# Copies, a gelu's scaling and row sums moved from VectorE to ScalarE in a one-core decode kernel

## The chip, the core and the metric

The kernel runs on one core of a Trainium2 chip. The metric is device microseconds of one execution, as the median of a few runs. All arithmetic is float32.

## What is computed

One decode step of a transformer block for 4 batch rows of one token each, width 512. The reference, cut to its core:

```python
mod = (silu(c) @ w_mod).reshape(4, 6, 1, 512)          # sa, ca, ga, sb, cb, gb
h = layernorm(x) * (1 + ca) + sa
q = (h @ wq) -> (4, 32 heads, 1, 128)
scores = q . k_cache * 128**-0.5                        # 8 kv heads, each for 4 q heads, 4096 keys
p = softmax(scores)
o = p . v_cache
x = x + ga * (o @ wo)                                   # wo: 4096 x 512
h = layernorm(x) * (1 + cb) + sb
z = layernorm(h)                                        # over the 512 columns
u = gelu(z[b, d] * w1[f] + b1[f])                       # f: 1792 hidden values per (b, d)
y = u . w2 + b2
out = x + gb * y
```

The key and value caches are 4 x 8 pairs of 2 MB + 2 MB, 134 MB together; with `w_mod`, `wq` and `wo` the kernel reads 157 MB.

## The kernel before

**Rows.** The work is cut into 32 rows `i`, one for each batch row `b = i // 8` and kv head `h = i % 8`. For row `i` the steps are small functions, each with a letter in the plan below:

- `scores` (line 226, PE): eight 512-wide matmuls into a PSUM tile `s` of 128 x 1024. The pool `ps_s` has two such buffers; the one of row `i` is free for row `i + 2` once the exponential of `i` has read it.
- the maximum: `row_max` on VectorE (line 236), `turn_max` (a transposition by PE into `pm`, line 240), `col_max` on VectorE (line 245), `spread_max` (PE into `pb`, line 251), and `copy_max` (line 256), which copies the 128 x 1 result from PSUM to the tile `nm`.
- `expo` (line 261, ScalarE): exponential with `nm` as bias, and with the sum of each partition accumulated; `turn` (VectorE, 32 x 32 block transpositions, whole at line 267 or in halves at line 271); `sums` (PE, `pl`, line 275) and `scale` (VectorE, reciprocal, line 280).
- `values` (PE, `pv`, line 291; the last rows use the narrow form at line 303), then `copy_v` (line 314), which copies the 128 x 512 result from PSUM to `po`; `pick` (PE, `pt`, line 328) and `copy_o` (VectorE, `oT`, line 335).
- `project` (PE with `wo`, `pa`, line 343) and `add_up` (line 359 copies the first projection of a batch row into `acc`, line 361 adds the others).

`pm`, `pb`, `pl`, `pt`, `pa` and the statistics `pst` share two PSUM buffers of the pool `ps_m`, in the order in which the program names them: each new one waits until the one two before has been read.

**Loads.** Keys and values come through a ring of three slots of 4 MB (`ring`), in pairs of keys `i + 2` and values `i`, all issued on SP's queue; a slot is loaded again once PE has consumed its values.

**The mixer.** The second half of the block for batch row `b` (class `Mixer`) runs beside the attention rows of `b + 1`. `expand` (VectorE, line 442) writes `hb * wr[:, j] + b1[:, j]` for two of 14 column groups `j` into a tile `u` of 128 x 1024, `gelu` (ScalarE, line 506) is applied to it, `consume` contracts it on PE (line 453). In the loop `both` does `expand` and `gelu`: in the rows with `i % 8` of 3 to 5 once between the two halves of `values` and in those of 2 to 5 once behind them. Mixers 0 and 1 run in the loop over rows 0 to 23. Mixer 2 runs in the plan below and mixer 3 in the closing sequence (`finish`); these use `expand` and `gelu` as separate steps.

**Gating of the last row.** The last batch row's residual is accumulated by PE itself: the `wo` columns of kv heads 6 and 7 are multiplied in place by the gate `ga` (`fold_gate`, line 592, letter `f`, eight products of 128 x 512), and the sum of each product goes into a column of `rowsum`, from which the mean for the layer norm is made.

**Order.** The order of the instructions on each engine is the order in which the program calls these functions (a manual schedule); each engine takes its list in order. Rows 0 to 23 come from the loop at line 618. From row 24 on the order is written out by hand in `PLAN` (line 667): for example `b31` is `spread_max(31)`, `B31` `copy_max(31)`, `e31` `expo(31)`, `t` a half of `turn`, `v` a quarter or half of `values`, `x` expand, `g` gelu, `c` consume, `f` one step of `fold_gate`, `L` followed by letters loads.

Of the kernel before, what the change touches and what calls it, by code (L numbers as in the profile page):

```python
# [8 lines left out]
F32 = mybir.dt.float32  # L9
AF = mybir.ActivationFunctionType  # L10
OP = mybir.AluOpType
# [3 lines left out]
B, D, HQ, HKV, SK, DH, F = 4, 512, 32, 8, 4096, 128, 1792  # L15
REP = HQ // HKV
NF = F // 128
EPS = 1e-5
P = 128
NS = B * HKV  # L20
# [8 lines left out]
def adaln_decode(ctx: ExitStack, tc: tile.TileContext, small, x, wmod, wq, kk, kv, vv, wo, out):  # L29
    nc = tc.nc  # L30
# [5 lines left out]
    up = ctx.enter_context(tc.tile_pool(name="up", bufs=3))  # L36
# [6 lines left out]
    dv = nc.vector  # L43
# [13 lines left out]
    w1, b1, w2 = sm[:, 0:NF], sm[:, NF:2 * NF], sm[:, 2 * NF:3 * NF]  # L57
# [34 lines left out]
    wo_t = [wo_p[h // 2][:, h % 2] for h in range(HKV)]  # L92
# [34 lines left out]
    for k in range(4):  # L127
        n = slice(k * P, (k + 1) * P)
# [95 lines left out]
    S, M, PL, RL = {}, {}, {}, {}  # L224
# [28 lines left out]

    def copy_max(i):
        nm = wk.tile([P, 1], F32, name="nm")
        dv.tensor_copy(nm, M[i])  # L256
        M[i] = nm

    def expo(i):
# [23 lines left out]
    PV, PA = {}, {}  # L283
# [27 lines left out]
    def copy_v(i):  # L311
        pv = PV[i]
        PV[i] = wk.tile(list(pv.shape), F32, name="po")
        dv.tensor_copy(PV[i], pv)  # L314

    ACC, OT = {}, {}

# [37 lines left out]
    def add_up(i):  # L355
        b, pa = i // HKV, PA.pop(i)
        if i % HKV == 0:
            ACC[b] = wk.tile([P, D], F32, name="acc", tag="acc", bufs=1)
            dv.tensor_copy(ACC[b], pa)
        else:  # L360
            dv.tensor_add(ACC[b], ACC[b], pa)  # L361

# [93 lines left out]
    class Mixer:  # L456
# [49 lines left out]
            nc.scalar.activation(u, u, AF.Gelu_apprx_tanh)  # L506
            self.done.append((u, js))

        def both(self, u=None):
            self.expand(u)  # L510
            self.gelu()

        def consume(self, most=9):
            if self.py is None:
# [65 lines left out]
    def spread_gate():  # L580
        pgb = ps_m.tile([P, 4, P], F32, name="pgb", tag="m")
        for c in range(4):
            e = 32 * c + 8 * (B - 1)
            mm(pgb[:, c, :], ident[:, e:e + 1].to_broadcast([P, P]), prep[:, 1], start=True, stop=True)
        gate = wk.tile([P, D], F32, name="gate", tag="yw", bufs=1)
        nc.scalar.activation(gate, pgb.rearrange("p c n -> p (c n)"), AF.Copy)
        return gate

    def fold_gate(gate, es):
        for e in es:  # L590
            w = wo_t[HKV - 2 + e // REP][:, e % REP]
            dv.tensor_tensor_reduce(w, w, gate, 1.0, 0.0, OP.mult, OP.add, rowsum[:, e:e + 1])

    rowsum = cst.tile([P, 2 * REP], F32, name="rowsum")
    tally = cst.tile([P, 2], F32, name="tally")
    both = cst.tile([P, 2 * REP], F32, name="both")
    mu = cst.tile([P, 1], F32, name="mu")

    def tally_up():
        junk = cst.tile([P, 2 * REP], F32, name="junk")  # L600
        dv.tensor_tensor_reduce(junk, both, rowsum, 1.0, tally[:, 0:1], OP.mult, OP.add, tally[:, 1:2])
# [10 lines left out]
    for i in range(2):  # L612
        for step in (scores, row_max, turn_max, col_max, spread_max, copy_max, expo):
            step(i)
# [3 lines left out]
    for i in range(NS - HKV):  # L618
# [13 lines left out]
        if i:  # L632
            project(i - 1)
            add_up(i - 1)
        turn_max(i + 2)
        col_max(i + 2)
        values(i, range(4))
        spread_max(i + 2)
        copy_max(i + 2)
        expo(i + 2)  # L640
        if i and i % HKV == 0:
            mix = Mixer(i // HKV - 1)
        if mix:
            mix.inner(i % HKV)
        values(i, range(4, 8))
        copy_v(i)
        if mix:
            mix.outer(i % HKV)
# [8 lines left out]
        if i == NS - HKV - 2:  # L657
            gate = spread_gate()
# [16 lines left out]
    g T2 zs za zx zq c c zm zb0 T3 zv zb1 zw0 zn zc  # L675
    """
    TABLE = {"s": scores, "S": row_max, "m": turn_max, "X": col_max, "b": spread_max, "B": copy_max, "e": expo,
             "l": sums, "L": scale, "V": copy_v, "a": pick, "A": copy_o, "P": add_up,
             "LP": load_pair}
    MIX = {"F": mix.fold, "R": mix.residual, "G": mix.gather, "M": mix.modulate, "H": mix.gather, "Q": mix.spread,  # L680
# [3 lines left out]
    for step in PLAN.split():  # L684
        op, k = step.rstrip("0123456789."), step.lstrip("abcdefghijklmnopqrstuvwxyzABCDEFGHIJKLMNOPQRSTUVWXYZ")
        i, q = (int(n) for n in (k + ".0").split(".")[:2]) if k else (0, 0)
# [25 lines left out]
        elif op == "x":  # L712
            mix.expand(spare if mix.n == 6 else None)
        elif op == "f":
            fold_gate(gate, gates[:1])
            del gates[:1]
        elif step == "T":
# [71 lines left out]
```

## Time and profile before

| | us |
|---|---|
| median of 3 runs | 386.43 |
| lowest and highest of them | 386.31, 390.96 |
| span of the profiled execution, first to last instruction | 384.7 |

| engine | busy us | share of the span |
|---|---|---|
| PE matmuls | 298.7 | 78% |
| PE weight loads | 117.2 | 30% |
| VectorE (DVE) | 198.2 | 52% |
| ScalarE (ACT) | 112.2 | 29% |
| GpSimd (POOL) | 7.7 | 2% |

The three runs and the profiled execution are separate executions; the span leaves out what lies around the first and the last instruction. In the page, PEld is PE's weight loading, which overlaps its matmuls, and "idle before" gives the time that an engine stood before an instruction and what released it. In the order of time a row reads: start, duration, engine, line, operation, output<-input, sizes, count, and in brackets the idle time with its releaser. In a stretch the columns are the busy time and count of PE, PEld, DVE, ACT, POOL, then the granted clock of PE, the DMA engines' mean busy share and their GB/s.

### The profile page before, as it was taken

Reading aid. Unit: us, or ns where it says so; the run is one execution under the profiler, and the core shown is the slowest. Engines: PE = TensorE matmul, PEld = TensorE weight load, DVE = VectorE, ACT = ScalarE, POOL = GpSimd, SP = SyncE. Lnnn points to the kernel's source line nnn. Section 1 sums busy time; section 2 is a strip of 40 time slices with the busy share of each in tenths; the row PEclk is TensorE's granted clock in tenths of the full one; section 3 lists DMA queues with packets and bytes.
Section 4 is the critical chain, followed back from the end, with each engine's and each line's share of the span. In section 5 each row is a group of like instructions: output and inputs, shape, how many; then the busy total and the mean of one; then the engine's idle time right before and its main releaser. Section 6 shows DMA issues by size and latency. Waiting matters only on the chain.

```text
span 384.7 us, 5604 instructions
## 1 busy us (share of the span) xinstructions
PE 298.7 (78%) x2380; PEld 117.2 (30%) x2380; DVE 198.2 (52%) x407; ACT 112.2 (29%) x144; POOL 7.7 (2%) x33
## 2 busy tenths in 40 slices
PE   0856777866966949979877878788888887999984
PEld 0112122311323313334322222342222343333653
DVE  1130251620451424664866545557665567778757
ACT  1001111121110110212567311124575105657276
POOL 1100000000000000000000000000000000000000
PEclk9989555985695685998999998999999999999999
DMA  8999999999999999999999999999999999999930
GB/s 331 433 433 436 411 453 433 409 432 436 423 441 433 434 436 436 434 436 431 429 425 433 428 433 434 429 433 431 429 434 436 434 436 432 424 417 423 418 122 3
DMA packets 7409, 157.69 MB, mean 410 GB/s; under 512 B 964, under 2 KB 1236, under 8 KB 1496
## 3 DMA queue, kind: packets, MB, share of 16 engines
q1 hardware_dynamic: 7376, 157.33, 95.4%
q8 instruction: 18, 0.29, 0.3%
q14 instruction: 7, 0.06, 0.0%
q10 hardware_dynamic: 8, 0.00, 0.0%
HBM read 157.32 MB, written 0.01 MB: 409 GB/s over the span
## 4 chain that ended last, share of the span: by engine, by line
DMA 60%; PE 29%; DVE 7%; ACT 2%; issue 1%; POOL 0%; SPq 0%; POOLq 0%; DVEq 0%
DMA kv<-in_kv 58%; PE s L231 8%; PE pv L291 7%; PE s L122 2%; PE qs L138 2%; DVE m L236 2%; DVE p L267 2%; DMA sm<-in_small 2%; PE pa L343 2%; PE pt L328 2%; ACT uu L562 1%; PE pb L251 1%; PE pve L303 1%; PE pm L240 1%; PE pgx L348 1%
## 5 line engine op out<-in xcount | busy, mean ns | idle before, releaser
L231 PE MATMUL s<-kv,QT 128*32 128x512 f32 x512 | 75.2, 714 | 38.9 <-DMA kv<-in_kv 37.0
L236 DVE TENSOR_REDUCE m<-s 128x1 f32<-128x1024 f32 x32 | 39.2, 1224 | 96.0 <-PE s L231 95.9
L261 ACT ACTIVATE p<-s,nm 128x1024 f32<-128x1024 f32 x32 | 35.7, 1115 | 180.6 <-DVE nm L256 180.5
L291 PE MATMUL pv<-kv,p 128*32 128x512 f32 x464 | 69.8, 670 | 0.7 <-DMA kv<-in_kv 0.7
L231 PEld LDWEIGHTS s<-kv,QT 128*32 128x32 f32 x512 | 15.8, 123 | 84.0 <-DMA kv<-in_kv 52.5
L328 PEld LDWEIGHTS pt<-g,po 128*128 128x128 f32 x236 | 31.1, 205 | 27.2 <-issue 19.9
L343 PE MATMUL pa<-wo,oT 128*32 128x512 f32 x240 | 34.6, 648 | 4.6 <-DVE oT L335 4.4
L328 PE MATMUL pt<-g,po 128*128 128x4 f32 (+2 forms) x236 | 33.9, 267 | 1.5 <-DVE po L314 1.0
L267 DVE STREAM_TRANSPOSE p<-p 128x1024 f32<-128x1024 f32 x25 | 30.9, 1234 | 0.0
L314 DVE COPY po<-pv 128x512 f32<-128x512 f32 x29 | 20.0, 688 | 16.8 <-PE pv L291 16.7
L245 DVE TENSOR_REDUCE mx<-pm 1x128 f32<-1x512 f32 x32 | 21.3, 669 | 1.1 <-PE pm L240 1.1
L442 DVE TENSOR_SCALAR u<-hb,wr,sm 128x512 f32<-128x512 f32 x40 | 19.9, 541 | 1.9 <-POOL wr L437 1.0
L506 ACT ACTIVATE u<-u 128x1024 f32<-128x1024 f32 x20 | 20.4, 1051 | 1.5 <-DVE u L442 1.4
L361 DVE TENSOR_TENSOR acc<-acc,pa 128x512 f32<-128x512 f32 x26 | 17.8, 686 | 4.3 <-PE pa L343 4.2
L261 ACT ACT_TABLE_LOAD x11 | 14.1, 1283 | 20.3 <-DVE nm L256 20.2
L251 PEld LDWEIGHTS pb<-neg,mx 1*128 1x128 f32 x64 | 10.4, 202 | 28.2 <-DVE mx L245 26.5
L122 PE MATMUL s<-wm,sT 128*4 128x512 f32 x16 | 9.1, 732 | 10.6 <-DVE sT L108 10.6
L506 ACT ACT_TABLE_LOAD x13 | 16.7, 1283 | 0.2
L291 PEld LDWEIGHTS pv<-kv,p 128*32 128x32 f32 x464 | 13.4, 146 | 7.2 <-issue 3.1
L240 PE MATMUL pm<-ident,m 128*1 128x128 f32 x32 | 9.3, 289 | 7.4 <-DVE m L236 3.5
L251 PE MATMUL pb<-neg,mx 1*128 1x1 f32 x64 | 13.1, 271 | 2.1 <-DVE mx L245 2.1
L453 PE MATMUL py<-u,sm 128*32 128x512 f32 x80 | 14.4, 616 | 0.0
(158 smaller groups left out, 214.7 us busy)
## 6 DMA issues: line engine op xcount, KB each, us to landing
kv<-in_kv SPq DMA_DIRECT2D x28, 4096.0 KB, 21.9
wq<-in_wq SPq DMA_DIRECT2D x2, 4096.0 KB, 16.3
wo<-in_wo SPq DMA_DIRECT2D x4, 2048.0 KB
kv<-in_kv SPq DMA_DIRECT2D x4, 2048.0 KB, 20.3
wm<-in_wmod SPq DMA_DIRECT2D x2, 2048.0 KB, 14.8
kv<-in_kk SPq DMA_DIRECT2D x1, 4096.0 KB
kv<-in_vv SPq DMA_DIRECT2D x3, 1024.0 KB
wm<-in_wmod SPq DMA_DIRECT2D x1, 1024.0 KB
```

The costliest lines, as they stand in the source:

```text
L231: mm(s[32 * c:32 * c + 32, n * 512:(n + 1) * 512], QT[:, b, h, :], KT[i][:, (n * 4 + c) * 512:(n * 4 + c + 1) * 512], start=True, stop=True)
L236: dv.tensor_reduce(M[i], S[i], axis=AX.X, op=OP.max)
L245: dv.tensor_reduce(mx, M[i].rearrange("o (c r) -> o r c", c=4).unsqueeze(1).to_broadcast([1, 4, 32, 4]), axis=AX.X, op=OP.max)
L251: mm(pb, M[i].rearrange("o c r -> o (c r)"), neg1, start=True, stop=True)
L261: nc.scalar.activation(p, S[i], AF.Exp, bias=M.pop(i), accum_out=l)
L267: dv.transpose(PL[i][0], PL[i][0])
L291: mm(PV[i][32 * q:32 * q + 32, :], pT[:, 128 * k:128 * k + 128:4], VT[i][:, 4 * k:4 * k + 4, :].rearrange("p j d -> p (j d)"), start=(k < ...
L314: dv.tensor_copy(PV[i], pv)
L328: mm(pt, po[:, c * DH:(c + 1) * DH], sel.unsqueeze(1).to_broadcast([P, m, REP]), start=(c == 0), stop=(c == n - 1))
L343: mm(pa[32 * g:32 * g + 32, :], oT[:, g:g + 1].to_broadcast([P, 32]), wo_t[h][:, g, :], start=True, stop=True)
L442: dv.tensor_scalar(u[:, e, :], hb, wr[:, j:j + 1], b1[:, j:j + 1], op0=OP.mult, op1=OP.add)
L506: nc.scalar.activation(u, u, AF.Gelu_apprx_tanh)
```

## The change

- `copy_max` (all 32 rows) runs on ScalarE.
- `copy_v` runs on ScalarE in rows 0 to 23; rows 24 to 31 stay on VectorE.
- The copy of the first projection of a batch row in `add_up` runs on ScalarE.
- `both` (mixers 0 and 1) no longer expands on VectorE: ScalarE applies gelu straight to `hb`, two instructions of 128 x 512 with `wr[:, j]` as scale and `b1[:, j]` as bias.
- `fold_gate`: in the first four of the eight steps VectorE multiplies two column groups (128 x 1024) by the gate, and in every step ScalarE copies one group of 128 x 512 in place and accumulates its sum. Before, each step was one product with sum on VectorE.

```diff
     def copy_max(i):
         nm = wk.tile([P, 1], F32, name="nm")
-        dv.tensor_copy(nm, M[i])
+        nc.scalar.activation(nm, M[i], AF.Copy)
         M[i] = nm
...
         PV[i] = wk.tile(list(pv.shape), F32, name="po")
-        dv.tensor_copy(PV[i], pv)
+        if i < NS - HKV:
+            nc.scalar.activation(PV[i], pv, AF.Copy)
+        else:
+            dv.tensor_copy(PV[i], pv)
...
         if i % HKV == 0:
             ACC[b] = wk.tile([P, D], F32, name="acc", tag="acc", bufs=1)
-            dv.tensor_copy(ACC[b], pa)
+            nc.scalar.activation(ACC[b], pa, AF.Copy)
...
-        def both(self, u=None):
-            self.expand(u)
-            self.gelu()
+        def both(self):
+            u = up.tile([P, 2, D], F32, name="u")
+            js = (2 * self.n, 2 * self.n + 1)
+            for e, j in enumerate(js):
+                nc.scalar.activation(u[:, e], self.hb, AF.Gelu_apprx_tanh, bias=b1[:, j:j + 1],
+                                     scale=self.wr[:, j:j + 1])
+            self.done.append((u, js))
+            self.n += 1
...
     def fold_gate(gate, es):
-        for e in es:
-            w = wo_t[HKV - 2 + e // REP][:, e % REP]
-            dv.tensor_tensor_reduce(w, w, gate, 1.0, 0.0, OP.mult, OP.add, rowsum[:, e:e + 1])
+        for n in es:
+            if n < REP:
+                w = wo_t[HKV - 2 + n // 2][:, n % 2 * 2:n % 2 * 2 + 2]
+                dv.tensor_mul(w, w, gate.unsqueeze(1).to_broadcast([P, 2, D]))
+            w = wo_t[HKV - 2 + n // REP][:, n % REP]
+            nc.scalar.activation(w, w, AF.Copy, accum_out=rowsum[:, n:n + 1])
```

The calls stand where they stood, so the order within each engine's list follows from the same loop and the same plan. At three places the lists are shown. First ScalarE in the plan, from the first gelu of mixer 2 to exponential 27 (`s27` is the scores of row 27), before:

```order
L506 ACT_TABLE_LOAD
L506 ACTIVATE u_1896<-u_1896 128x1024
L261 ACT_TABLE_LOAD
L261 ACTIVATE p_1929,l_1930<-s26_1833,nm_1927 128x1024
L506 ACT_TABLE_LOAD
L506 ACTIVATE u_1908<-u_1908 128x1024
L506 ACTIVATE u_1932<-u_1932 128x1024
L261 ACT_TABLE_LOAD
L261 ACTIVATE p_2008,l_2009<-s27_1887,nm_1949 128x1024
```

and now (line 603 is a row sum of `fold_gate`, 362 the first projection's copy, 256 a copied maximum, 509 the gelu):

```order
L603 ACTIVATE wo6_131,rowsum_236<-wo6_131 128x512
L509 ACT_TABLE_LOAD
L509 ACTIVATE u_1882<-u_1882 128x1024
L362 ACTIVATE acc_1904<-pa_1889 128x512
L256 ACTIVATE nm_1914<-pb_1912 128x1
L261 ACT_TABLE_LOAD
L261 ACTIVATE p_1916,l_1917<-s26_1819,nm_1914 128x1024
```

```order
L509 ACT_TABLE_LOAD
L509 ACTIVATE u_1895<-u_1895 128x1024
L256 ACTIVATE nm_1936<-pb_1922 128x1
L509 ACTIVATE u_1919<-u_1919 128x1024
L603 ACTIVATE wo6_131,rowsum_236<-wo6_131 128x512
L261 ACT_TABLE_LOAD
L261 ACTIVATE p_1996,l_1997<-s27_1873,nm_1936 128x1024
```

The copy of the first projection now follows a row sum and a gelu, and exponential 27 follows a second row sum. The second place is ScalarE between exponentials 30 and 31, before:

```order
L261 ACT_TABLE_LOAD
L261 ACTIVATE p_2145,l_2146<-s30_2066,nm_2135 128x1024
L261 ACTIVATE p_2169,l_2170<-s31_2113,nm_2166 128x1024
L506 ACT_TABLE_LOAD
L506 ACTIVATE u_2132<-u_2132 128x1024
```

and now:

```order
L261 ACT_TABLE_LOAD
L261 ACTIVATE p_2134,l_2135<-s30_2055,nm_2124 128x1024
L603 ACTIVATE wo6_131,rowsum_236<-wo6_131 128x512
L256 ACTIVATE nm_2156<-pb_2150 128x1
L603 ACTIVATE wo6_131,rowsum_236<-wo6_131 128x512
L261 ACTIVATE p_2159,l_2160<-s31_2102,nm_2156 128x1024
L603 ACTIVATE wo6_131,rowsum_236<-wo6_131 128x512 x2
L509 ACT_TABLE_LOAD
L509 ACTIVATE u_2121<-u_2121 128x1024
```

Two row sums and the copied maximum now stand between the two exponentials, and two more row sums behind. The third place is VectorE at the same time, from row maximum 31 to the copy of values 28, before:

```order
L236 TENSOR_REDUCE m_2137<-s31_2113 128x1
L361 TENSOR_TENSOR acc_1917<-acc_1917,pa_2127 128x512
L245 TENSOR_REDUCE mx_2149<-pm_2143 1x128
L592 ISA wo6_131,rowsum_236<-wo6_131,gate_1739 128x512
L592 ISA rowsum_236 128x1
L256 COPY nm_2166<-pb_2160 128x1
L592 ISA wo6_131,rowsum_236<-wo6_131,gate_1739 128x512
L592 ISA rowsum_236 128x1
L314 COPY po_2179<-pv_2151 128x512
```

and now:

```order
L236 TENSOR_REDUCE m_2126<-s31_2102 128x1
L364 TENSOR_TENSOR acc_1904<-acc_1904,pa_2116 128x512
L245 TENSOR_REDUCE mx_2138<-pm_2132 1x128
L601 TENSOR_TENSOR wo6_131<-wo6_131,gate_1725 128x1024
L317 COPY po_2169<-pv_2140 128x512
```

One product of 1024 columns (line 601) replaces two products with sums and the copied maximum; the row sum that stands first on ScalarE's list above reads what this product writes.

## Prediction

> **What bounds the kernel now.** I read the slices and the chain of waits first, then the stretches of five microseconds, then the order of time in the last 70 us.
>
> ```profile
> DMA  8999999999999999999999999999999999999930
> DMA 60%; PE 29%; DVE 7%; ACT 2%; issue 1%; POOL 0%; SPq 0%; POOLq 0%; DVEq 0%
> kv<-in_kv SPq DMA_DIRECT2D x28, 4096.0 KB, 21.9
> SPq L176 <- PE pv L291: 186.4, 23, 12.3
> ```
>
> Each digit of the first row is a fortieth of the span: the DMA engines are full from the start to slice 37. The chain gives them 60%. A pair of 4 MB takes 21.9 us from issue to landing, while a pair's own transfer is about 9.7 us (4.19 MB at some 430 GB/s; the stretches quoted below move 383 to 446), so at each issue about 12 us of older loads are still under way. The last row is SP waiting for a free buffer. A row of the loop may therefore be late by some 12 us before the loads starve. For most of the program a faster VectorE or a slower ScalarE is worth nothing.
>
> The end is another matter.
>
> ```profile
> 343.17 1.92 PE L231 MATMUL s<-kv,QT 128*32 128x512 f32 x16 [0.60 <-DMA kv<-in_kv]
> 362.58 0.81 PEld L303 LDWEIGHTS pve<-kv,p 128*32 128x32 f32 x32 [0.86 <-DMA kv<-in_vv]
> 362.58 1.08 PE L303 MATMUL pve<-kv,p 128*32 128x128 f32 x32
> 367.23 0.14 PEld L303 LDWEIGHTS pve<-kv,p 128*32 128x32 f32 x4 [0.17 <-DMA kv<-in_vv]
> ```
>
> Scores 30 start when their keys land; PE had waited 0.60 us for them. From there PE is hardly ever idle: the matmuls at 362.58 carry no idle time (only the weight loads waited), and the last piece of values makes the weight loads wait 0.17 us. Loads and computation end together; after 367.4 only the closing sequence of 17 us is left. So a delay between 343 and 367 goes into the time almost in full, a gain there is worth 0.2 us at most, and a delay before 343 is paid only beyond the 0.60 us.
>
> **The change, part by part.** Durations first.
>
> ```profile
> L314 DVE COPY po<-pv 128x512 f32<-128x512 f32 x29 | 20.0, 688 | 16.8 <-PE pv L291 16.7
> L218 ACT ACTIVATE ym<-pm 128x512 f32<-128x512 f32 x3 | 1.8, 597 | 7.8 <-PE pm L215 7.8
> L256 DVE COPY nm<-pb 128x1 f32<-128x1 f32 x32 | 5.0, 156 | 16.1 <-PE pb L251 16.0
> L731 ACT ACTIVATE tab<-ones 1x1 f32<-1x1 f32 x1 | 0.2, 202 | 0.0
> L506 ACT ACTIVATE u<-u 128x1024 f32<-128x1024 f32 x20 | 20.4, 1051 | 1.5 <-DVE u L442 1.4
> L557 ACT ACTIVATE uu<-hb,sm,wr 128x512 f32<-128x512 f32 x2 | 1.5, 806 | 0.1
> L261 ACT ACT_TABLE_LOAD x11 | 14.1, 1283 | 20.3 <-DVE nm L256 20.2
> L442 DVE TENSOR_SCALAR u<-hb,wr,sm 128x512 f32<-128x512 f32 x40 | 19.9, 541 | 1.9 <-POOL wr L437 1.0
> L592 DVE CUSTOM_DVE_ANT_0 wo<-wo,gate 128x512 f32<-128x512 f32 x8 | 5.4, 677 | 0.0
> L568 DVE TENSOR_TENSOR osb<-osb,xk 128x384 f32<-128x384 f32 x1 | 0.6, 558 | 0.0
> L371 DVE TENSOR_TENSOR xk<-xk,prep 128x128 f32<-128x128 f32 x3 | 0.9, 291 | 0.1
> ```
>
> A copy of values costs 0.60 us on ScalarE (the ym row has its shape and source) instead of 0.69. A copy of a maximum costs about 0.20 us there instead of 0.16. A scaled gelu of two columns is 2 x 0.806 = 1.61 us on ScalarE instead of 1.05, and frees 2 x 0.54 on VectorE. The trace has no 1024-wide product: from 128 to 384 columns the two TENSOR_TENSOR rows grow by 267 ns per 256, so 1024 take 558 + 2.5 x 267 = 1.23 us; I bound it by 0.62 (half that rate) and 1.35 (two of 0.677). A row sum on ScalarE is a copy from SBUF, 1.05 less 0.43 for half the columns = 0.62, and 0.19 for reading the accumulator (row below): 0.81 us; between 0.60 (nothing to read) and 1.0.
>
> *Rows 0 to 23.* In a row with a gelu on both sides ScalarE's list is now maximum 0.20, table load 1.28, exponential 1.31, table load 1.28, gelus 1.61, values 0.60, gelus 1.61: 7.9 us against a period of 9.7. The copy of values sits behind the inner gelus, about 6.2 us after the maximum; PE's pick, the oT product and the transposition of the next row follow it, so a loop from maximum to maximum forms in three rows of each of two mixers: 6.2 + 1.1 for the pick + 1.4 for transposing two halves (0.69 each, row below) + some 1.7 for turning and spreading the maximum with half a row's values between, an estimate of 10.4 us. Each such row loses some 0.7 us, and the first 1 to 1.5 us more: 3 to 4 us of the 12 that the queued loads cover. Cost 0; without that cover it would be those 3 to 4 us.
>
> *From 319 to 343.* Here the first row sum and the first copy of a projection (P24) enter ScalarE's list around a gelu.
>
> ```profile
> 320.01 0.68 DVE L592 CUSTOM_DVE_ANT_0 wo<-wo,gate 128x512 f32<-128x512 f32 x1
> 320.10 1.06 ACT L506 ACTIVATE u<-u 128x1024 f32<-128x1024 f32 x1
> 323.76 0.27 PE L240 MATMUL pm<-ident,m 128*1 128x128 f32 x1 [0.88 <-DVE acc L359]
> 332.17 1.11 ACT L261 ACTIVATE p<-s,nm 128x1024 f32<-128x1024 f32 x1
> 333.15 0.68 DVE L592 CUSTOM_DVE_ANT_0 wo<-wo,gate 128x512 f32<-128x512 f32 x1
> 337.04 0.69 DVE L271 STREAM_TRANSPOSE p<-p 128x512 f32<-128x512 f32 x1
> ```
>
> The third row shows PE waiting for P24 already, since the turned maximum needs its PSUM buffer. Now ScalarE does that copy, in its order behind row sum and gelu: product until 320.0 + 1.23 = 321.25, sum 322.1, table load 323.35, gelu 324.4, P24 325.0. PE goes on at 325.05, 1.3 us later. Then the second row sum stands ahead of the table load and exponential 27, and its product stands behind the row maximum of scores 28 on VectorE (333.15 in the trace, about 1 us later now): 334.15 + 1.23 + 0.81 + 1.28, so the exponential moves from 332.17 to about 337.5. It lasts 1.11, and its transposition stood at 337.04, so of these 5 us only 1.5 arrive. The loads, 12 us of which are queued, do not notice buffers freed 1.3 us later. The 0.60 us for which PE waited before scores 30 and the idle of PE's weight loads on the way take up most of the 1.3 to 1.5; at worst all but 0.2 of it stays (1.3), at best nothing (0). I take 0.4, nearer to nothing since the load and not the computation set that start.
>
> *Exponential 31.* This is the main term.
>
> ```profile
> 352.86 0.68 DVE L245 TENSOR_REDUCE mx<-pm 1x128 f32<-1x512 f32 x1 [0.17 <-PE pm L240]
> 353.80 0.38 PE L251 MATMUL pb<-neg,mx 1*128 1x1 f32 x2
> 354.21 0.16 DVE L256 COPY nm<-pb 128x1 f32<-128x1 f32 x1
> 354.47 1.11 ACT L261 ACTIVATE p<-s,nm 128x1024 f32<-128x1024 f32 x1 [0.92 <-DVE nm L256]
> 355.48 0.19 ACT L261 ACTIVATION_READ_ACCUMULATOR p<-s,nm 128x1 f32 x1
> 355.73 0.38 PE L275 MATMUL pl<-g,l 128*128 128x4 f32 x2 [0.21 <-ACT p L261]
> ```
>
> PE already waits 0.21 us for exponential 31, and behind this matmul stand pick 28, projection 28 and all of values 29 to 31. In the new order ScalarE has, between exponentials 30 and 31, row sum 3 (counted from 0), the maximum, row sum 4. Row sum 3 waits for VectorE's product, which starts after the column maximum at 353.54 and ends at 354.77; sum 3 ends at 355.58, the maximum at 355.78, sum 4 at 356.59. Exponential 31 starts then instead of at 354.47: +2.1 us (1.5 to 2.6 by the bounds above). Nothing hides it: PE has only the sum of row 30 to do meanwhile.
>
> *Behind it.* VectorE loses its later row sums of 0.68 us, but its next steps there wait for PE; the loads that come due at 362.58 and 367.23 will now have landed, which pays back the 0.17. The sums that follow exponential 31 on ScalarE stand ahead of gelus only, which PE consumes after values 31. The closing sequence is unchanged. 0.
>
> Sum: 0 + 0.4 + 2.1 = +2.5 us. The span of 384.7 becomes 387.2. The median of the three runs, 386.43, is 1.7 above the span, so 388.9 us, which is 0.65% more. 2% is about what a measurement of this kernel can tell from no change.
>
> **Rivals.** *The clock falls into the new gap.* PE would be idle from about 355.5 (355.73 less its wait) to 358.2.
>
> ```profile
> PEclk9989555985695685998999998999999999999999
> 320.00:325.00 5.00, 3.59 (x33) 1.20 (x25) 4.73 (x12) 1.15 (x2) 0.00 (x0) 1.00 0.97 419
> 325.00:330.00 5.00, 5.00 (x26) 1.43 (x30) 2.90 (x7) 4.92 (x6) 0.00 (x0) 0.66 1.03 446
> 98.22 1.80 PE pt L328 x8
> 100.45 1.87 PE pa L343 x8
> 347.33 1.13 PE pt L328 x8
> 357.52 1.07 PE pa L343 x8
> ```
>
> The sixth number of a stretch, after POOL's, is the granted clock. It fell to 0.66 on average after a stretch with 3.59 us of 5 busy. At half clock a pick took 1.80 and a projection 1.87 instead of 1.13 and 1.07, so one such spell behind the gap costs about 0.7 + 0.8 less what lies outside it: +1.3, and 390.2 us. Against it: by the first row, in fortieths of the span, the clock stayed at 9 tenths or more in every slice from the 26th on, with gaps in many of them, so falls are short and few by then.
>
> The Trainium skill (TensorE: Matmul & The Clock Gate, Part 1: The HAM clock gate) says the gate closes after a whole idle window of about 3.4 us; by that rule a gap of 2.7 us would never do it and the time stays 388.9. The stretch from 320 to 330 does not agree, since it had no idle of that length.
>
> *Not slower: the loads come forward.* If VectorE's relief frees the early buffers sooner, holes in the loads close.
>
> ```profile
> 45.00:50.00 5.00, 2.88 (x14) 0.33 (x6) 1.90 (x2) 0.32 (x2) 0.00 (x0) 0.50 0.95 410
> 70.00:75.00 5.00, 3.92 (x33) 1.26 (x30) 1.33 (x4) 1.21 (x2) 0.00 (x0) 1.00 0.91 383
> ```
>
> The DMA share (last but one) is short by 0.05 and 0.09 of 5 us: 0.7 us in all; only if keys 30 landed 2.5 us sooner, before 340.6, would the time stay at 386.4. Holes of that sum are not in the trace.
>
> *ScalarE bounds the mixer rows.* Were the loop there 13 us instead of 10.4, six rows would use up the 12 us and more: some 8 us slower, past 394. The list of 7.9 us speaks against it.
>
> **How the numbers follow.** Forecast 388.9: 0.50, of itself 388.0 to 389.9 (main term 1.5 to 2.6, the stretch before it 0 to 1.3). Clock falls, 390.2: 0.30. Loads come forward, 386.4: 0.13. Mixer rows, over 394: 0.07. Leaving out the last and some of the edges, the range is 386.3 to 391.2. Only the mixer rows pass 2%: faster 0.01, within 0.92, slower 0.07.
>
> **What would show it.** Right: exponential 31 some 13.4 us after scores 30 instead of 11.3, with ScalarE's row sums directly ahead of it; the sum matmul of row 31 (355.73 now) waiting over 2 us for ScalarE; P24 ending 1.3 us later; weight loads of the last values without a wait for DMA; the DMA row unchanged to slice 37. Wrong: a span not above 385.2 us, a wait of that matmul below 1 us, loads with holes in rows 10 to 22, or row sums far from 0.81 us and products far from 1.23.

## The result, and the profile after

| | before | after |
|---|---|---|
| median of 20 runs, us | 386.47 | 393.99 |
| lowest and highest, us | 386.31, 390.96 | 387.88, 400.12 |
| profiled execution, us | | 387.88 |
| its span, us | 384.7 | 386.1 |

The ratio of the times is 1.0106 with a 95% interval of 1.0072 to 1.0140: about 1% slower, 390.6 us beside the forecast of 388.9. That ratio leaves out runs more than 1.5% above the fastest of their kernel, 11 of the 20 here, while the ratio of the medians of all runs, 393.99 / 386.47 = 1.019, is the one that a user would see. So the changed kernel is slower by 1 to 2%, and its runs spread over 12 us where 16 of the 20 of before lie within 0.4 us. The spread needs an explanation as much as the shift does.

The page of the changed kernel, from its shortest run:

```profile
span 386.1 us, 5605 instructions
PE 296.3 (77%) x2380; PEld 117.0 (30%) x2380; DVE 162.1 (42%) x307; ACT 143.6 (37%) x234; POOL 7.7 (2%) x33
...
PEclk9989765697896979958978799999999999899999
DMA  8999999999999999999999999999999999999910
...
DMA 33%; PE 29%; issue 17%; ACT 11%; DVE 8%; POOL 1%; SPq 0%; POOLq 0%; DVEq 0%
```

36.1 us left VectorE (198.2 before) and 31.4 came to ScalarE (112.2). The DMA row is full to slice 37 as before: no load starved. But in the chain that ended last ScalarE went from 2% to 11%, DMA from 60% to 33%, and "issue" (time in which an engine waited for nothing that the profile shows) from 1% to 17%. So work of ScalarE now stands on the path for a long way. Where, the groups tell:

```profile
L331 PE MATMUL pt<-g,po 128*128 128x4 f32 (+2 forms) x236 | 33.4, 265 | 10.0 <-ACT po L315 9.5 <-DVE rl L280 0.5
L516 ACT ACTIVATE u<-hb,sm,wr 128x512 f32<-128x512 f32 x28 | 21.2, 804 | 0.1
L315 ACT ACTIVATE po<-pv 128x512 f32<-128x512 f32 x24 | 14.1, 586 | 3.2 <-PE pv L291 3.2
L256 ACT ACTIVATE nm<-pb 128x1 f32<-128x1 f32 x32 | 5.5, 170 | 152.8 <-PE pb L251 152.7
L603 ACT ACTIVATE wo<-wo 128x512 f32<-128x512 f32 x8 | 5.0, 622 | 3.0 <-DVE wo L601 3.0
L601 DVE TENSOR_TENSOR wo<-wo,gate 128x1024 f32<-128x1024 f32 x4 | 4.8, 1212 | 0.0
L603 ACT ACTIVATION_READ_ACCUMULATOR wo<-wo 128x1 f32 x8 | 1.5, 190 | 0.0
```

The first row is the new wait: PE's pick (line 331) stood 9.5 us for the copy of values (line 315), in 7 rows, up to 2.5 us each. Before, it waited for that copy for 1.0 us in all, in two picks of the plan and in none ahead of it. The other rows give the prices.

In order of time, the copies of values in rows 12 and 13, in which the first mixer runs, with what surrounds them; after and then before:

```profile
205.50 1.28 ACT L516 ACT_TABLE_LOAD   x1
206.79 1.52 ACT L516 ACTIVATE u<-hb,sm,wr 128x512 f32<-128x512 f32 x2
208.22 0.57 ACT L315 ACTIVATE po<-pv 128x512 f32<-128x512 f32 x1
208.85 1.05 PE L331 MATMUL pt<-g,po 128*128 128x4 f32 x8 [1.75 <-ACT po L315]
...
211.68 1.94 PE L291 MATMUL pv<-kv,p 128*32 128x512 f32 x8
...
219.60 0.57 ACT L315 ACTIVATE po<-pv 128x512 f32<-128x512 f32 x1
```

```profile
198.82 0.69 DVE L314 COPY po<-pv 128x512 f32<-128x512 f32 x1
...
208.58 0.69 DVE L314 COPY po<-pv 128x512 f32<-128x512 f32 x1
```

The copy waits on ScalarE behind a table load of 1.28 us and two gelus of 1.52 us together, PE waits for the copy, and from copy to copy pass 11.4 us instead of 9.8; the copy of row 13 is 11.0 us late. Behind PE's wait its clock also fell (0.61 granted from 210 to 215 us): the half of the values at 211.68 took 1.94 us, where the same eight matmuls take 1.09 at full clock. In rows 19 to 21, those of the second mixer, the clock stayed at 1.00, and the copies began at 272.14, 282.38 and 292.63, 10.2 us apart. What becomes of that lag is seen at VectorE's row maxima (line 236), here those of rows 16, 19, 25 and 26, after and then before:

```profile
219.69 1.22 DVE L236 TENSOR_REDUCE m<-s 128x1 f32<-128x1024 f32 x1 [7.12 <-PE s L231]
...
243.54 1.22 DVE L236 TENSOR_REDUCE m<-s 128x1 f32<-128x1024 f32 x1 [1.41 <-PE s L231]
...
303.60 1.22 DVE L236 TENSOR_REDUCE m<-s 128x1 f32<-128x1024 f32 x1 [2.59 <-PE s L231]
318.03 1.22 DVE L236 TENSOR_REDUCE m<-s 128x1 f32<-128x1024 f32 x1
```

```profile
212.97 1.23 DVE L236 TENSOR_REDUCE m<-s 128x1 f32<-128x1024 f32 x1 [2.47 <-PE s L231]
...
243.55 1.22 DVE L236 TENSOR_REDUCE m<-s 128x1 f32<-128x1024 f32 x1 [3.37 <-PE s L231]
...
302.06 1.22 DVE L236 TENSOR_REDUCE m<-s 128x1 f32<-128x1024 f32 x1 [2.59 <-PE s L231]
316.61 1.21 DVE L236 TENSOR_REDUCE m<-s 128x1 f32<-128x1024 f32 x1
```

Row 16 is 6.7 us late, row 19 not at all: the first mixer's lag is made good while the loads stay queued, as predicted. The second mixer's lag is 1.5 us at row 25 and still 1.4 at row 26, where the hand-written plan has begun; the span is 1.4 longer. On balance nothing is made good between row 25 and the end.

The plan itself, in order of time:

```profile
322.67 0.63 ACT L603 ACTIVATE wo<-wo 128x512 f32<-128x512 f32 x1 [2.47 <-DVE wo L601]
325.66 0.58 ACT L362 ACTIVATE acc<-pa 128x512 f32<-128x512 f32 x1
326.29 0.27 PE L240 MATMUL pm<-ident,m 128*1 128x128 f32 x1 [2.57 <-ACT acc L362]
...
344.74 1.92 PE L231 MATMUL s<-kv,QT 128*32 128x512 f32 x16
...
354.97 0.62 ACT L603 ACTIVATE wo<-wo 128x512 f32<-128x512 f32 x1
...
355.04 1.20 DVE L601 TENSOR_TENSOR wo<-wo,gate 128x1024 f32<-128x1024 f32 x1
...
356.44 1.10 ACT L261 ACTIVATE p<-s,nm 128x1024 f32<-128x1024 f32 x1
357.69 0.38 PE L275 MATMUL pl<-g,l 128*128 128x4 f32 x2 [0.62 <-ACT p L261]
```

The first projection's copy (P24) holds PE up for 2.57 us instead of 0.88, as the order had it. Scores 28 start 2.26 us late (331.37 against 329.11), scores 30, for whose keys PE no longer waits 0.60 us, at 344.74, 1.57 late. The main term of the prediction is in the last four rows: row sum 3 of ScalarE began at 354.97, before the product of VectorE at 355.04 that it was to wait for. It does not read what that product writes; the text on the third list and the prediction both have that wrong. Exponential 31 comes 11.70 us after scores 30 and not 13.4, and the sum matmul behind it waits 0.62 us and not over 2.

### The profile page after: what moved, and what is told of

The parts are those of the page before. It is cut to its first block, busy times and chain, and to the rows that moved or that the text cites. A ratio compares the mean times of both kernels' runs of the same rounds, so it can differ in the third digit from the quotient of the medians.

```text
span 386.1 us, 5605 instructions
## 1 busy us (share of the span) xinstructions
PE 296.3 (77%) x2380; PEld 117.0 (30%) x2380; DVE 162.1 (42%) x307; ACT 143.6 (37%) x234; POOL 7.7 (2%) x33
## 4 chain that ended last, share of the span: by engine, by line
DMA 33%; PE 29%; issue 17%; ACT 11%; DVE 8%; POOL 1%; SPq 0%; POOLq 0%; DVEq 0%
DMA kv<-in_kv 31%; PE pv L291 8%; PE s L231 6%; PE pt L331 3%; DVE m L236 2%; DVE p L267 2%; ACT u L516 2%; PE qs L138 2%; PE s L122 2%; ACT p L261 2%; ACT L516 2%; ACT L261 2%; DMA sm<-in_small 2%; PE pa L346 2%; PE pb L251 2%
## 5 line engine op out<-in xcount | busy, mean ns | idle before, releaser
L291 PE MATMUL pv<-kv,p 128*32 128x512 f32 x464 | 72.9, 698 | 0.0
L256 ACT ACTIVATE nm<-pb 128x1 f32<-128x1 f32 x32 | 5.5, 170 | 152.8 <-PE pb L251 152.7
L516 ACT ACTIVATE u<-hb,sm,wr 128x512 f32<-128x512 f32 x28 | 21.2, 804 | 0.1
L122 PE MATMUL s<-wm,sT 128*4 128x512 f32 x16 | 8.5, 689 | 10.2 <-DVE sT L108 10.2
L315 ACT ACTIVATE po<-pv 128x512 f32<-128x512 f32 x24 | 14.1, 586 | 3.2 <-PE pv L291 3.2
L240 PEld LDWEIGHTS pm<-ident,m 128*1 128x1 f32 x32 | 2.5, 79 | 38.2 <-DVE rl L280 26.3
```

The source lines that it names most:

```text
L122: mm(s0[0:B, t * D:(t + 1) * D], sT[:, k, :], wm01[:, t, k, :], start=(k == 0), stop=(k == 3))
L291: mm(PV[i][32 * q:32 * q + 32, :], pT[:, 128 * k:128 * k + 128:4], VT[i][:, 4 * k:4 * k + 4, :].rearrange("p j d -> p (j d)"), start=(k < ...
L516: nc.scalar.activation(u[:, e], self.hb, AF.Gelu_apprx_tanh, bias=b1[:, j:j + 1], scale=self.wr[:, j:j + 1])
```

## The experiments

The first theory after this reading, the loop: the copy of values, behind the gelus, sets the pace of the mixer's rows, and the lag of rows 19 to 23 goes into the plan. Rivals: the plan's own part (P24, row sums), the loads, and the clock as the cause in itself. Each kernel is the changed one with the edit shown; medians are over all runs of it (6 or 12), ratios are against the kernel before.

**The copies of values back on VectorE.**

```diff
-        if i < NS - HKV:
-            nc.scalar.activation(PV[i], pv, AF.Copy)
-        else:
-            dv.tensor_copy(PV[i], pv)
+        dv.tensor_copy(PV[i], pv)
```

> All copies of values back on VectorE, the rest as in the change. If the loop through ScalarE's copy of values in the mixer rows costs the time (the copy stands behind the inner gelus, 11.4 us from copy to copy against 9.7 us a pair of loads), the median falls from 394.0 to 386.5 to 388.0 and the runs agree within 2 us. If the plan's row sums and copies of maxima cost it, the median stays over 391 with the same spread of 12 us.

Median 387.2 us, span 384.6 in the profile, ratio 1.0020 (0.9989 to 1.0051). Of the 7.5 us between the medians all but 0.7 is gone with this one edit; the gelus with scale, the copied maxima and the row sums stayed on ScalarE. The runs did not come together within the 2 us that were expected: two of the twelve took 390.7 us, and one took 883 us, for which there is no trace.

**The same work on ScalarE in another order**: in the three rows the inner gelus are issued behind the copy of values instead of ahead of it.

```diff
-        if mix:
+        if mix and i % HKV < 3:
             mix.inner(i % HKV)
         values(i, range(4, 8))
         copy_v(i)
+        if mix and i % HKV >= 3:
+            mix.inner(i % HKV)
```

> As the change, with the same work on ScalarE, but in rows of the mixer with inner gelus these are issued behind the copy of values instead of ahead of it. Loop theory: the copy comes 1.6 to 2.9 us earlier in each such row, the loop is 7.5 us and the median is 386.5 to 388.0, runs within 2 us. Theory that ScalarE's amount of work in these rows is too much: no change, 392 to 395.

Median 387.79 us, ratio 1.0020 (0.9995 to 1.0045), with runs from 386.43 to 390.27. ScalarE is as busy as in the changed kernel (143.6 us in both), so its amount of work is not what costs. Its copies of values:

```profile
200.45 0.59 ACT L315 ACTIVATE po<-pv 128x512 f32<-128x512 f32 x1
210.11 0.59 ACT L315 ACTIVATE po<-pv 128x512 f32<-128x512 f32 x1
```

They stand 9.7 us apart again, at the period of the loads, and PE's picks wait 1.0 us in all instead of 9.5. The cause in rows 0 to 23 is the place of the copy in ScalarE's list.

**The gelu's scaling back on VectorE, the copy left where it was.**

```diff
-        def both(self):
-            u = up.tile([P, 2, D], F32, name="u")
...
-            self.n += 1
+        def both(self, u=None):
+            self.expand(u)
+            self.gelu()
```

> As the change, but the scaling ahead of gelu is back on VectorE, so an inner gelu holds ScalarE for 1.05 instead of 1.61 us. The copy of values stays behind it. Loop theory: the loop is 9.8 us at full clock, hardly above a pair's 9.7, so most of the loss goes: 387 to 390 with a smaller spread. Plan theory: unchanged, over 391.

A miss: 393.19 us, ratio 1.0150 (1.0094 to 1.0206), no better than the changed kernel. The loop itself came out as expected, 9.8 us from copy to copy at 271.76 and 281.59, with the copy still behind a table load and a gelu. PE waited less for the copy (5.0 us in five rows), yet the span of its profile is 390.1. A stretch of it:

```profile
295.00:300.00 5.00, 4.84 (x27) 1.25 (x27) 1.75 (x4) 1.62 (x3) 0.00 (x0) 0.53 1.05 452
```

PE was busy for 4.84 of 5 us at a granted clock of 0.53, with the DMA engines full: it was slow, not idle. In this profile a good part of the lag is the clock's, and not that of the waits alone.

**The gating back on VectorE.**

```diff
-        for n in es:
-            if n < REP:
...
-            nc.scalar.activation(w, w, AF.Copy, accum_out=rowsum[:, n:n + 1])
+        for e in es:
+            w = wo_t[HKV - 2 + e // REP][:, e % REP]
+            dv.tensor_tensor_reduce(w, w, gate, 1.0, 0.0, OP.mult, OP.add, rowsum[:, e:e + 1])
```

> As the change, but the gating with its row sums is back on VectorE as before. Loop theory: only the 0.4 us of exponential 31 and some of exponential 27 come back; median 392 to 395 with the spread of the change. Plan theory (the forecast's main term): 2 us or more come back in every run, lowest run 386.5 or below.

Median 391.43 us, ratio 1.0088 (1.0055 to 1.0122), in two groups: four runs from 387.13 to 388.56, eight from 391.39 to 392.43. With the row sums gone not one of the twelve reached 386.5, so the plan's row sums are not the main cause. They have a part in it, though: the median fell by 2.6 us, and the spread from 12 to 5 us. The two groups asked for a second profile of this kernel, below.

**Which rows matter.** One kernel copies on VectorE from row 18 on, the other only in rows 10 to 15.

```diff
-        if i < NS - HKV:
+        if i < 2 * HKV + 2:
```

> As the change, but from row 18 on, the rows of the second mixer in the loop, the copy of values is on VectorE; rows 0 to 17 keep it on ScalarE. Theory now: only the second mixer's delay counts, since the plan that begins with row 24 has no slack to make it good, and the first mixer's is made good in rows 14 to 18: median 386.5 to 388.5, as with all copies back. Rival, that the loads starve wherever the 12 us of queued loads are used up (the first mixer's delay was the larger one, 6.7 us): 390 to 394.

```diff
-        if i < NS - HKV:
+        if i < HKV + 2 or 2 * HKV <= i < NS - HKV:
```

> The reverse: the copy of values on VectorE in rows 10 to 15 only, the rows of the first mixer; on ScalarE in rows 0 to 9 and 16 to 23. Theory now: nothing gained, median 391 to 395 with the change's spread. Rival, starving loads: 386.5 to 388.5.

With the copies of the second mixer's rows on VectorE: 387.78 us, ratio 1.0019 (0.9994 to 1.0044). With those of the first mixer's rows: 392.15 us, ratio 1.0100 (1.0067 to 1.0132), the same as the whole change. The lag of rows 10 to 15, the larger of the two, costs nothing that these medians show; 6.2 of the 7.5 us are those of the last mixer's rows ahead of the plan. That also speaks against the loads as the main cause: a starved load would not care which mixer had made PE late. A single run in which they did starve follows below.

**Keeping PE busy.** Scores of rows 21 to 25 are computed a second time into the same tile, to keep PE from pausing; the output is unchanged.

```diff
         scores(i + 2)
+        if i > 2 * HKV + 2:
+            scores_again(i + 2)
```

> As the change, but in rows 19 to 23 of the loop PE computes the eight score matmuls of the next but one row a second time, into the same buffer, ahead of the row maximum. PE then has no pause in which its clock can fall, at the price of 1.9 us of PE time in a row of 9.7. If the falling clock in PE's waits for the copy of values makes the long runs, the spread shrinks and the median is 388 to 391, below the change's 394. If the loop alone does it, the added PE work makes it no better: 394 or more, same spread.

A miss as a remedy: 396.53 us, ratio 1.0249 (1.0196 to 1.0303). Its profile, of the shortest run, shows a granted clock of 1.00 in every stretch of 5 us from 270 to 325, and the copies of values in rows 19 to 21 starting at 274.1, 284.3 and 294.6: 10.2 us apart, as in the changed kernel at full clock. Yet row 25's maximum came at 307.25, 5.2 us later than before the change, presumably because the 1.9 us of added scores a row take up time that PE had for catching up. So the experiment cannot tell what the falls of the clock cost, and leaves that question where it was.

**The gating kernel once more, for a second profile.**

> The kernel with the gating back on VectorE once more, for a profile: its runs came in two groups, 387.1 to 388.6 and 391.4 to 392.4, and the profile fell in the lower one. Two in three runs fall in the upper one. In such a profile the clock theory expects half clock somewhere in rows 19 to 24 (270 to 300 us), a copy of values 21 to 23 over 2 us later than in the lower group, and loads that land as before until row 24. A theory of starving loads expects holes in the loads instead.

It took 389.85 us, between the two groups, with a span of 388.1 against 385.3 in the first profile. The two runs of one and the same program are level at row 24 (its maximum at 291.8 and 291.5). Then, in the first and the second run, the pick of row 21 and the next 5 us:

```profile
293.00 1.05 PE L331 MATMUL pt<-g,po 128*128 128x4 f32 x8 [1.27 <-ACT po L315]
```

```profile
295.00:300.00 5.00, 3.97 (x35) 1.16 (x35) 2.41 (x5) 2.78 (x5) 0.00 (x0) 1.00 1.02 439
```

```profile
293.26 1.63 PE L331 MATMUL pt<-g,po 128*128 128x4 f32 x8 [1.82 <-ACT po L315]
```

```profile
295.00:300.00 5.00, 5.00 (x25) 1.42 (x29) 2.59 (x5) 0.09 (x1) 0.00 (x0) 0.50 1.05 452
```

After a wait of 1.27 us the clock stayed at 1.00, after one of 1.82 it fell to 0.50, and the last matmuls of that pick are slow already (1.63 us for 1.05). Row 25's maximum then came at 307.8 instead of 303.4, and of these 4.4 us 2.8 reached the end of the span. The other 1.6 were lost in the first run too, one row later, in a spell of its own (0.66 granted from 310 to 315).

**What is left without the last mixer's copies.** The last mixer's copies on VectorE (as in the kernel with the change from row 18 on), and in addition P24 there, or the gating, or both.

```diff
-            nc.scalar.activation(ACC[b], pa, AF.Copy)
+            if b < B - 1:
+                nc.scalar.activation(ACC[b], pa, AF.Copy)
+            else:
+                dv.tensor_copy(ACC[b], pa)
```

> As with the copy of values on VectorE from row 18 on (387.8 median, 386.4 to 389.1), and the copy of the last batch row's first projection back on VectorE too. Theory: what is left of the spread is PE's pause of 2.6 us for that copy, behind a row sum, a table load and a gelu on ScalarE, after which the clock sometimes falls for two windows; without it the median is 386.4 to 386.9. Rival, row sums ahead of exponentials 27 and 31 on ScalarE: unchanged, 387.3 to 388.2.

> As with the copy of values on VectorE from row 18 on, and the gating with its row sums back on VectorE, while the copy of the first projection stays on ScalarE. Pause theory: that copy then stands behind a table load and a gelu only, 0.8 us earlier, and the pause shrinks but does not go: 386.6 to 387.6. Rival of the row sums: 386.4 to 386.8.

> Both edits together: copies of maxima, the copies of values of rows 0 to 17, three first projections and the mixers' scaling stay on ScalarE. Both theories: as before the change, median 386.3 to 386.7. A median above 387 would mean that the copies of maxima or the mixers' scaling cost something of their own. A gain is not expected, since the loads' end and the closing sequence are untouched.

| on VectorE from row 18 on | median, us | ratio |
|---|---|---|
| copies of values | 387.78 | 1.0019 (0.9994 to 1.0044) |
| and P24 | 387.21 | 1.0026 (1.0004 to 1.0048) |
| and the gating | 386.55 | 1.0014 (0.9994 to 1.0035) |
| and both | 386.57 | 1.0004 (0.9990 to 1.0018) |

With P24 alone the forecast was missed; with the gating alone the median lies 0.05 us below the forecast and within that of the rival, the row sums. With both moved the kernel is as fast as before, although all maxima and the values of rows 0 to 17 are still copied on ScalarE and the first two mixers' scaling is still done there: these parts of the change cost nothing in the median, and gain nothing. How the rest, about 1 us in the median, divides between P24 and the row sums stays open, since the intervals overlap. Some of the spread does not lie in the program at all: the profiled execution of the first of these four kernels took 388.03 us with a span of 384.6. The profile of the third was of its longest run but one (393.14 us, span 391.4; the longest took 436 us, without a trace), and shows two things that no other profile here shows so late:

```profile
230.00:235.00 5.00, 4.42 (x42) 1.98 (x42) 3.08 (x7) 0.27 (x1) 0.00 (x0) 1.00 0.77 328
...
315.00:320.00 5.00, 4.80 (x28) 2.00 (x32) 2.81 (x9) 0.00 (x0) 0.55 (x1) 0.50 1.03 446
```

Here the first mixer's lag did reach the loads. PE had waited 1.99 and 2.49 us for copies of values at 209 and 221 us, the copy of row 14 came 11.4 us later than before the change, the next pair of loads was issued 13.0 us after the one ahead of it (228.59 and 215.63), and the DMA engines moved only 328 GB/s from 230 to 235; the row maxima are 1.2 us late from row 20 to row 24. At 312.0 PE then waited 1.51 us for values still in transfer, and from 313.3 to 330.4 us the clock stayed at half, with PE hardly ever idle after 315.

**The changed kernel once more, for a longer run.**

> The changed kernel once more, for one more profile: the first was of its shortest run (span 386.1 us), and most of its runs are 4 to 8 us longer. Clock theory: if this run is a longer one, its transfers land when they did before (the last piece of values within 0.5 us of 367 us), the extra time lies in stretches of 5 us after 244 us in which PE is busy for 4.5 us or more at a granted clock of 0.5 to 0.7, and each such spell begins after one or two waits of PE for the copy of values or for the first projection's copy that sum to about 2 us. Rival, the loads: the extra time lies in the transfers themselves, the last pieces of values landing later by as much as the span is longer, with a lower DMA share in some stretch. If it is a run at the lower end again (span below 388), nothing is told apart.

It took 390.47 us with a span of 388.7, 2.6 more than in the first profile. Rows of its order of time, then two stretches of it and the last one with loads:

```profile
270.49 1.92 PE L231 MATMUL s<-kv,QT 128*32 128x512 f32 x16 [1.61 <-DMA kv<-in_kv]
273.10 1.06 PE L331 MATMUL pt<-g,po 128*128 128x4 f32 x8 [0.68 <-ACT po L315]
...
294.72 1.06 PE L331 MATMUL pt<-g,po 128*128 128x4 f32 x8 [2.49 <-ACT po L315]
...
306.22 1.22 DVE L236 TENSOR_REDUCE m<-s 128x1 f32<-128x1024 f32 x1 [2.59 <-PE s L231]
```

```profile
275.00:280.00 5.00, 5.00 (x27) 1.21 (x23) 1.85 (x4) 1.55 (x3) 0.00 (x0) 0.52 1.00 429
...
295.00:300.00 5.00, 5.00 (x32) 1.96 (x34) 2.66 (x5) 1.07 (x2) 0.00 (x0) 0.66 1.05 452
...
365.00:370.00 5.00, 4.70 (x116) 3.36 (x112) 3.12 (x11) 0.00 (x0) 0.00 (x0) 1.00 0.64 256
```

The same three stretches of the first profile:

```profile
275.00:280.00 5.00, 3.79 (x35) 1.20 (x35) 1.49 (x4) 2.99 (x5) 0.00 (x0) 1.00 0.99 423
...
295.00:300.00 5.00, 4.13 (x35) 1.07 (x27) 2.55 (x5) 2.53 (x4) 0.00 (x0) 1.00 1.06 459
...
365.00:370.00 5.00, 4.70 (x122) 3.96 (x110) 2.50 (x10) 2.11 (x2) 0.00 (x0) 1.00 0.65 259
```

The last row of each settles the rival for these two runs: the loads end at the same place (259 and 256 GB/s in the 5 us in which they end; 156 of the 157.7 MB had been moved at 364.1 us in both), while row 25's maximum came 2.6 us later (306.22 against 303.60) and the end of the span by as much. The clock theory holds with one correction. The spell from 275 began behind a wait of 0.68 us for the copy and, 2 us before that, one of 1.61 us for keys: the pauses need not all be ScalarE's. The spell from 295 began behind the copy alone, 2.49 us. In the first profile a pick at the same place had waited 1.80 us and the clock held.

These profiles reach 390.5 us for the changed kernel. That its runs from 393.5 to 400 us are more spells of the same kind, some of them with a hole in the loads like the one above, is argued from them and from the other kernels' profiles, and was not seen.

## Why the prediction was right, and where it was wrong

The forecast of 0.65% slower stands beside a measured 1.06%, inside the range and on the right side; the median of all runs, 394.0, is outside it. The sum came out near for the wrong reasons.

*"Rows 0 to 23 ... Cost 0"* is the step that failed. The loop was seen (an estimate of 10.4 us; 10.2 measured at full clock, 11.4 and 12.2 with spells at half clock), its cover was seen too, and in both profiles of the changed kernel the cover does what was said: the loads did not starve, and the first mixer's 6.7 us (3 to 4 forecast) vanished by row 19. What was not asked is how much of the program is left after the lag for it to be made good. Scores 21 to 24 still wait for their keys, and there the copies' lag (5.3 us at row 21, 292.63 against 287.33) is hidden. From scores 25 on the plan keeps PE near its limit, and before the change PE waited for loads there only for 0.20, 0.52 and 0.60 us; what is left of the lag goes to the end almost whole (1.5 us at row 25 and 1.4 in the span; in the longer run 4.2 and 4.0). The text had all it needed: it said that a delay before 343 is paid only beyond the 0.60 us for which PE waited there, and did not set the 3 to 4 us of this loop against those 0.60.

*"Exponential 31: +2.1"* was mis-sized. Row sum 3 was taken to read what the product of the same number writes. But a product covers two column groups: sum 3 reads the second group of product 1, written some 19 us before (335.42), and only sums 0 and 2 had to wait for the product that they read (products 0 and 1; 2.47 and 0.57 us). From scores 30 to exponential 31 it was 11.70 us against 11.3, so +0.4 for two row sums of 0.81 us ahead of it. The lower bound of 1.5 was too high in itself: with product and row sums both at their lowest (0.62 and 0.60 us) the same addition gives 1.1. Nor do the two ranges, 1.5 to 2.6 and 0 to 1.3, add up to "388.0 to 389.9", but to 387.9 to 390.3.

*From 319 to 343: +0.4.* P24's wait was seen, 2.57 us in place of 0.88, with PE resuming at 326.29 where 325.05 was forecast; the 1.4 us of lag brought along were not in that forecast. Exponential 27 started at 334.89 and not at 337.5, by the same error as above: row sum 1 read the second group of product 0 and had no product to wait for. The further cost of this stretch in the shortest run is small, 1.57 at scores 30 against 1.4 at row 26, and the 0.60 us of cover were used as forecast. What was not counted is the clock. Behind this pause it fell in the shortest run (0.72 from 325 to 330), as it had before the change (0.66), and in the kernel with the inner gelus behind the copy for longer,

```profile
325.00:330.00 5.00, 4.44 (x17) 1.39 (x18) 3.43 (x6) 4.68 (x6) 0.00 (x0) 0.54 1.03 446
```

with a wait of 2.03 us before it and a span of 386.0. The kernel with copies on VectorE from row 18 on comes to this place at the same time (row 26's maximum at 316.33 and 316.39) with the same plan, waited 2.00 us, kept its clock, and has a span of 384.6. So in these two profiles the plan's own part of the change cost nothing where the clock held, and 1.4 us where it fell.

*The prices* were right: copy of values 0.60 forecast, 0.586 measured; product 1.23 and 1.21; row sum 0.81 and 0.62 + 0.19; two gelus 1.61 and 1.61; copied maximum 0.20 and 0.17.

*The rivals.* "The clock falls into the new gap" came true as a mechanism, though not in its place: the gap before the sum of row 31 was 0.62 us, and the falls that counted came in rows 19 to 25 and behind P24. "ScalarE bounds the mixer rows", past 394, had 0.07; the loop measured 10.2 to 12.2 us rather than 13, the loads starved in one of the profiles (of another kernel), and yet the median of all runs, 393.99, lies at its edge. "Loads come forward" did not show: the last stretch of loads before moved 266 GB/s, after 259, 35 KB less, which is 0.1 us at 430 GB/s.

## What to carry to other kernels

Work that moves to an engine with time to spare takes that engine's place in line: ask what stands ahead of each moved instruction in its list and who waits for it, not how busy the engine is; two orders of the same work differed here by 6 us in the median. A lag is covered only if something behind it still has idle time to give back, so follow it to the next stretch without any. And where PE works close to its loads, price its waits not by their length alone: here a wait of some 2 us could cost one or more spells of half clock, in some runs and not in others, so look at the spread of all runs and not at a median alone.

## What the runs showed of the hardware

The granted clock of PE fell to half behind waits much shorter than the spell that followed: in the longer runs quoted above behind one of 1.82 us, one of 2.49, and the pair of 1.61 and 0.68. It held behind single ones of 1.27 and 1.80. The length of one wait does not decide it alone: behind P24's wait of 2.00 us in the kernel with the change from row 18 on it held, and in the one with P24 on VectorE it fell behind a wait of 1.04 us,

```profile
323.99 0.27 PE L240 MATMUL pm<-ident,m 128*1 128x128 f32 x1 [1.04 <-DVE acc L365]
```

```profile
325.00:330.00 5.00, 4.73 (x24) 1.67 (x28) 3.00 (x7) 4.94 (x7) 0.00 (x0) 0.66 1.00 433
```

as it had in the kernel before, behind 0.88 us. The same program has the fall in one run and not in the next, at the same place.

The clock records of these traces show a part of the reason. In each trace the spells at half clock begin whole multiples of 3.41 us apart, as on a grid of steps. From 160 us to the end of the loads they last one to five steps (3.4 us to the 17.1 told above), though PE was busy for most of the time. How busy PE was in the step before goes with it: between 160 and 360 us of the 14 traces, those of both kernels and of the experiments, the clock fell behind all 23 steps in which PE was busy for less than 40% of the time, behind 26 of 107 with 40 to 70%, and behind 7 of 596 above that. So it matters where a wait lies on this grid. The wait of 2.03 us for P24 (322.62 to 324.65) lay within one step, 322.02 to 325.43, in which PE was busy for 34%, and the clock fell at its end; that of 2.00 us (322.59 to 324.59) was divided by the step's end at 323.99 into two steps with 59 and 66%, and the clock held. The share is no sharp threshold, and why the clock stays at half for several steps with PE busy stays open.

The Trainium skill (TensorE: Matmul & The Clock Gate, Part 1: The HAM clock gate) puts the fall after a whole idle window of about 3.4 us, and says that the window runs freely, so that one kernel is caught differently in different runs. The second agrees with the grid of 3.41 us and with the two profiles each of the changed kernel and of the gating kernel. The first does not: none of the waits named here was that long.
